# Attention and gated mixer on one core: P.V in bursts of two waves, seven P slots beside in-place VectorE tiles, the polynomial in halves, and unread products on TensorE

## The chip, the cores and the metric

The kernel runs on one core of one Trainium2 chip. The metric is device time in microseconds (us) of one execution, as the median of several runs. The core has four engines that matter here: TensorE (PE in the profile; PEld is its weight load), VectorE (DVE), ScalarE (ACT) and GpSimd (POOL); SyncE (SP) issues transfers. Each engine works through its own instructions in order, and semaphores tie the engines together.

## The reference: what is computed

Two branches over the same 2048 x 512 input x, mixed by a gate per row. All tensors are bfloat16.

```
A:  q = x @ wq (32 heads of 16),  k = x @ wk,  v = x @ wv      (one k and v for all heads)
    p = softmax(q k^T / 4),  a = concat(p v) @ wo
B:  z = gelu(x @ w_in);  z1 = z[:, :688];  z2 = layernorm(z[:, 688:])
    b = (z1 * (w_sp @ z2 + b_sp)) @ w_out
out = g * a + (1 - g) * b,   g = sigmoid(sum(x * gate_w))
```

The bulk is branch A: 32 heads x 2048 x 2048 scores, their exponentials, and the products of these with v.

## The kernel before

**Units and blocks.** The heads and queries are cut into 32 units. A unit takes four groups g (0 to 3) of 32 partitions, each group with its own head's 512 queries, against 2048 keys in 16 tiles of 128. That makes 64 blocks a unit, 2048 in all, each of 128 keys x 512 queries. For one block:

- TensorE makes the scores (`s_mm`): 32 rows of the array by 128 columns; blocks of different g run side by side as one wave, up to four.
- The exponential is taken by ScalarE, or by VectorE with a polynomial.
- TensorE multiplies by v (`pv_mm`): 128 rows by 32 columns, again up to four blocks of different g in a wave, summed for the unit in PSUM bank BO.

All matmuls with a tile position are issued on line 276, full ones (128 x 128) on line 275.

**ScalarE's path.** Steps alternate between three and two blocks, in two sets of PSUM banks (three banks, two banks). Line 539 takes the exponential of a whole step into one of NP = 5 slots of the tile P. A slot is free again when P.V has read its blocks.

**VectorE's path.** It takes blocks in batches of four. Each block's scores come through one PSUM bank, BD. Line 563 (`d_A`) reads the bank, scales and shifts it into a quarter of X. After four such steps the whole batch goes through three instructions (`d_poly`): line 570 squares X in place, line 571 adds a constant in place, line 572 squares X into the tile PD. The result is the polynomial's value; a correction per unit (two waves of products with MC and CC) makes good what the polynomial leaves out. X has NX = 3 slots, PD has ND = 4. A new batch (`new_batch`) starts only if the third last batch is computed and the fourth last is read by P.V.

**The end of a unit** (`norm`): VectorE transposes bank BO (line 582), takes the reciprocal of the sums (583), multiplies (585, 586) and after every second unit transposes the result (590). The next unit's P.V waits for line 582, since BO is single.

**The other work** ("misc"): projections, the two halves of z, the mixing with w_sp, and the output products. All of it goes through one PSUM bank, BM, in groups: a few full products, then one VectorE instruction that empties the bank. ScalarE's gelu passes run in one stretch, once all of z is there; in that stretch no exponentials run.

**What sets the order.** The order of each engine's instructions is fixed when the program is built. A planner steps through time with estimated costs: at each moment it takes, for the engine that is free first, the ready candidate with the lowest priority number. On TensorE these are the scores of ScalarE's next step (0), P.V under pressure (0.5), scores for VectorE alone (1), P.V or a correction (2), misc (3). Scores for VectorE's bank are added to the wave of ScalarE's step where the bank is free, or go alone if ScalarE's next step isn't due "soon". P.V goes if at least four blocks are ready, if the oldest unread P slot is about to hold up ScalarE ("press"), or if the unit is at its end ("last"). On VectorE the order is emptying of BM, `norm`, other work, `d_A`, polynomial. How many batches VectorE gets is not set by hand: it follows from the plan, within limits per unit (at most seven batches of a unit's 16). When the chip is slower than the plan's costs, the order stays and the semaphores make the engines wait.

## Time and profile before

| | us |
|---|---|
| median of 3 runs | 876.12 (874.2 to 879.94) |
| the profiled execution's own time | 871.82 |
| its span, first to last instruction | 870.0 |
| mean granted TensorE clock | 0.92 |
| busy: TensorE, ScalarE, VectorE | 798.3, 810.5, 665.8 |
| batches of four on VectorE | 89 |

The profile is of one execution. A row of a group reads: line, engine, operation, tile written <- tiles read, shapes, count | busy us, mean ns of one | idle time of the engine before them, and what ended it. A line of a timeline reads: start, length, engine, line, operation, tiles, count of instructions that are merged into it. A window reads: from:to, length, then busy time and count for each engine, the granted TensorE clock (1.00 is full speed), and DMA. Ends of matmuls are modelled, so the distance from start to start says more than the length. Since a window counts each instruction that touches it, counts at its edges are rough.

### The profile page before, as it was taken

What the parts mean: (1) busy time and instruction counts of PE and PEld (TensorE: products, weight loads), DVE (VectorE), ACT (ScalarE), POOL (GpSimd) and SP (SyncE); (2) the same over time, 40 slices, a digit from 0 to 9 for tenths busy, and PEclk for the clock granted to TensorE, in tenths of its full rate; (3) what the DMA queues carried; (4) which work ended last, traced back from release to release, by engine and by line L of the source; (5) the groups of instructions that cost most, each with busy time, mean ns of one, the idle gap of its engine ahead of it and who ended that gap; (6) DMA issues with size and microseconds to landing.
All of it is one profiled execution on the core that took longest, in us unless ns stands there. A gap on an engine that the chain in (4) does not pass through costs nothing.

```text
span 870.0 us, 13369 instructions
## 1 busy us (share of the span) xinstructions
PE 798.3 (92%) x5270; PEld 228.7 (26%) x5347; DVE 665.8 (77%) x1014; ACT 810.5 (93%) x698; POOL 10.9 (1%) x17
## 2 busy tenths in 40 slices
PE   8989999999990999999999999999989999999996
PEld 2222322222220122222222222222222222221222
DVE  3678888788989876877887888878668777867662
ACT  6889999999999789999999999999999999999893
POOL 2000000000000100000000000000000000000000
PEclk9789999999995599999999999999979999995757
DMA  9600000000000000004000031000050000000000
GB/s 235 119 1 1 1 2 1 1 2 2 1 1 0 2 1 1 1 6 105 13 2 1 1 80 36 7 2 1 1 98 13 13 1 1 2 1 1 1 2 28
DMA packets 49048, 16.98 MB, mean 20 GB/s; under 512 B 44129, under 2 KB 48913, under 8 KB 48978
## 3 DMA queue, kind: packets, MB, share of 16 engines
q1 hardware_dynamic: 46210, 15.23, 7.9%
q8 instruction: 44, 0.72, 0.4%
q10 hardware_dynamic: 2640, 0.56, 0.3%
q0 software_dynamic: 128, 0.26, 0.2%
q14 instruction: 26, 0.21, 0.1%
HBM read 3.20 MB, written 2.10 MB: 6 GB/s over the span
## 4 chain that ended last, share of the span: by engine, by line
PE 64%; DVE 25%; issue 6%; ACT 4%; ACTq 0%
PE ps L276 44%; PE ps L275 20%; DVE X L563 6%; DVE X L570 4%; ACT P L539 4%; DVE PD L572 3%; DVE bst L467 2%; DVE X L571 2%; DVE T L582 1%; DVE z L453 1%; DVE Tn L586 1%; DVE QA L341 1%; DVE z L477 1%; DVE OT L590 1%; DVE z L446 0%
## 5 line engine op out<-in xcount | busy, mean ns | idle before, releaser
L539 ACT ACTIVATE P<-ps 128x1536 bf16<-128x1536 f32 (+1 forms) x677 | 784.2, 1245 | 37.9 <-PE ps L276 32.7
L276 PE MATMUL ps<-QA,KA 32*128 32x512 bf16 x2048 | 327.3, 408 | 43.4 <-DVE X L563 23.5
L563 DVE TENSOR_SCALAR X<-ps 128x512 f16<-128x512 f32 x356 | 243.8, 685 | 131.6 <-PE ps L276 131.3
L276 PE MATMUL ps<-P,V 128*32 128x512 bf16 x1692 | 285.1, 416 | 2.0 <-DVE T L582 1.2
L276 PEld LDWEIGHTS ps<-QA,KA 32*128 32x128 bf16 x2048 | 78.5, 92 | 282.7 <-ACT P L539 120.7
L275 PE MATMUL ps<-wT,z 128*128 128x512 bf16 x351 | 113.9, 390 | 3.6 <-issue 2.9
L570 DVE TENSOR_TENSOR X<-X 128x2048 f16<-128x2048 f16 x89 | 108.9, 1223 | 2.6
L572 DVE TENSOR_TENSOR PD<-X 128x2048 bf16<-128x2048 f16 x89 | 108.7, 1221 | 1.9
L276 PEld LDWEIGHTS ps<-P,V 128*32 128x32 bf16 x1692 | 67.1, 94 | 163.4 <-issue 155.3
L571 DVE TENSOR_SCALAR X<-X 128x2048 f16<-128x2048 f16 x89 | 61.0, 685 | 0.6
L276 PE MATMUL ps<-PD,V 128*32 128x512 bf16 x356 | 46.3, 418 | 5.7 <-DVE PD L572 4.4
L275 PEld LDWEIGHTS ps<-wT,z 128*128 128x128 bf16 x384 | 29.6, 98 | 58.2 <-issue 51.0
L582 DVE STREAM_TRANSPOSE T<-ps 128x512 f32<-128x512 f32 x32 | 22.7, 711 | 16.9 <-PE ps L276 16.9
L275 PE MATMUL ps<-win,xT 128*128 128x344 bf16 x128 | 30.3, 315 | 2.5 <-DVE z L453 1.3
L275 PE MATMUL ps<-wout,z 128*128 128x512 bf16 x87 | 27.1, 392 | 1.4 <-issue 0.7
L275 PE MATMUL ps<-xT,win 128*128 128x512 bf16 x87 | 26.7, 384 | 1.6 <-DVE z L446 0.5
L500 DVE TENSOR_TENSOR z<-ps,z 128x512 bf16<-128x512 f32 (+1 forms) x24 | 16.4, 683 | 6.0 <-PE ps L276 4.2
L276 PE MATMUL ps<-QA,MC 128*32 128x512 bf16 x128 | 20.0, 428 | 0.5 <-DVE ct L422 0.5
L276 PE MATMUL ps<-ones,CC 128*32 128x512 bf16 x128 | 19.8, 427 | 0.0
L275 PE MATMUL ps<-xT,wq 128*128 128x512 bf16 x55 | 17.9, 385 | 1.1 <-DVE z L453 0.6
L275 PE MATMUL ps<-wo,OT 128*128 128x512 bf16 x59 | 18.6, 384 | 0.0
L446 DVE CAST z<-ps 128x512 bf16<-128x512 f32 x24 | 16.4, 683 | 1.7 <-PE ps L275 1.7
(97 smaller groups left out, 265.0 us busy)
## 6 DMA issues: line engine op xcount, KB each, us to landing
out_dram<-outsb SPq DMA_DIRECT2D x16, 128.0 KB, 1.7
win<-in_B_w_in_dram SPq DMA_DIRECT2D x2, 688.0 KB, 5.5
wout<-in_B_w_out_dram SPq DMA_DIRECT2D x1, 640.0 KB, 9.0
wo<-in_A_wo_dram SPq DMA_DIRECT2D x1, 512.0 KB, 6.6
wq<-in_A_wq_dram ACTq DMA_DIRECT2D x1, 384.0 KB, 7.4
wT<-in_B_w_sp_dram SPq DMA_TRANSPOSE x16, 4.5
KA<-KA POOLq DMA_DIRECT2D x4, 64.0 KB, 2.7
wq<-in_A_wq_dram ACTq DMA_DIRECT2D x1, 128.0 KB, 3.9
```

Of the source, the lines that this page charges most:

```text
L275: return t.matmul(dst, lhsT, rhs, start=start, stop=stop)
L276: return t.matmul(dst, lhsT, rhs, start=start, stop=stop, tile_position=tp)
L341: [(620, lambda: op("dve", lambda v: v.tensor_copy(QA[:, qt % NQ, :], bank(BM)), r=[BMK], w=[("Q", qt % NQ)], tag="Qev"))],
L446: ev = lambda: op("dve", lambda v: v.tensor_copy(z1[:, ft, 512 * tc:512 * tc + 512], bank(BM)), r=[BMK], w=[("z1", ft)], tag="z1ev")
L467: dve_q.append((440, lambda st=st, h=h: op("dve", lambda v: v.bn_stats(bst[:, st, h, :], z2[:, FH * st + 344 * h:FH * st + 344 * h + 344]) ...
L500: ev = lambda: op("dve", lambda v: v.tensor_tensor(dst, ps[0:n, 512 * BM:512 * BM + 512], dst, ALU.mult), r=[BMK, ("z1", ft)], w=[("u", ft ...
L539: op("act", lambda a: a.activation(P[:, k % NP, 0:512 * n], ps[:, 512 * b0:512 * (b0 + n)], ACT.Exp), r=[("sc", k % 2)], w=[("P", k % NP)] ...
L563: op("dve", lambda v: v.tensor_scalar(X[:, m % NX, 512 * i:512 * i + 512], bank(BD), PA, PB, ALU.mult, ALU.add), r=[("bk", BD)], w=[("X", ...
L570: (C2, lambda: op("dve", lambda v: v.tensor_tensor(x, x, x, ALU.mult), r=[k], w=[k], tag="dU")),
L571: (C4, lambda: op("dve", lambda v: v.tensor_scalar(x, x, PC, None, ALU.add), r=[k], w=[k], tag="dV")),
L572: (C2, lambda: op("dve", lambda v: v.tensor_tensor(PD[:, m % ND, :], x, x, ALU.mult), r=[k], w=[("PD", m % ND)], tag="dW")),
L582: res = [(660, lambda: o("dve", lambda v: v.transpose(T1[:], bank(BO)), r=[("bk", BO)], w=["T1"], tag="T1"), setT(("O", u)))]
```

## The change

1. **P.V in bursts of two waves.** P.V goes if eight blocks are ready (PVMIN), no longer four. "Press" now sets in when NP - PRESS = 6 slots back is reached (five slots unread), with NP = 7; before it was NP - 2 = 3 (two slots unread).
2. **Seven P slots; VectorE's tiles in place.** P goes from 5 to 7 slots. PD is gone: the last step of the polynomial writes bfloat16 over the float16 values it reads, in X, which has 5 slots. A new batch starts if the fifth last is read.
3. **The polynomial in halves.** Each of the three instructions over 2048 elements becomes two over 1024, in the order square, square, add, add, last square, last square. X is tracked by halves, and the first half's two blocks can go to P.V ahead of the second's.
4. **The plan's costs.** A TensorE candidate is charged 105 ns where its kind (S scores, P P.V, M full products) differs from the one before; before, it was 100 for each S and P and 60 in front of misc. The costs of VectorE's polynomial are those of the halves. "Soon" is 300 ns, no longer 500.
5. **Unread products.** `load` keeps for the last 3400 ns of the plan how much of the array the matmuls used (a full product of 512 columns counts 1, a score or P.V product 1/4). If TensorE has nothing to do within 100 ns, bank BM is free and the sum is under KEEP = 6.5, `keep_pick` issues a product of ones with ones into BM that nobody reads. While the gelu passes run, it also waits for the newest VectorE instruction.

```diff
-NP = 5
-NX = 3
-ND = 4
+NP = 7
+NX = 5
...
+PVMIN = 8
+PRESS = 1
+SOON = 300
+KEEP = 6.5
...
-        PD = sb("PD", [128, ND, 512 * DB], B16)
...
-        def mm(dst, lhsT, rhs, start, stop, r, w, tp=None, tag=""):
+        def mm(dst, lhsT, rhs, start, stop, r, w, tp=None, tag="", after=()):
...
+            load.append((T["now"], lhsT.shape[0] * sh[0] * n / (128.0 * 128 * 512)))
+            return op("pe", fn, r=r, w=w, after=after, tag=tag)
...
-        C512, C344 = 220.0, 150.0
-        C4, C2 = 80 + 0.26 * 512 * DB, 75 + 0.5208 * 512 * DB
+        C512, C344 = 218.0, 148.0
+        SW = 105.0
+        C4, C2 = 40 + 0.26 * 256 * DB, 30 + 0.5208 * 256 * DB
...
         def d_poly(m):
-            x = X[:, m % NX, :]
-            k = ("X", m % NX)
-            return [
-                (C2, lambda: op("dve", lambda v: v.tensor_tensor(x, x, x, ALU.mult), r=[k], w=[k], tag="dU")),
-                (C4, lambda: op("dve", lambda v: v.tensor_scalar(x, x, PC, None, ALU.add), r=[k], w=[k], tag="dV")),
-                (C2, lambda: op("dve", lambda v: v.tensor_tensor(PD[:, m % ND, :], x, x, ALU.mult), r=[k], w=[("PD", m % ND)], tag="dW")),
-            ]
+            res = []
+            hw = 512 * DB // 2
+            pair = [(X[:, m % NX, hw * h:hw * h + hw], ("X", m % NX, h), X[:, m % NX, hw * h:hw * h + hw].bitcast(B16), ("X", m % NX, h)) for h in range(2)]
+            for x, k, p_, kp in pair:
+                res.append((C2, lambda x=x, k=k: op("dve", lambda v: v.tensor_tensor(x, x, x, ALU.mult), r=[k], w=[k], tag="dU")))
...
-            if m >= NX and bdone.get(m - NX) is None:
-                return False
-            if m >= ND and pd_left.get(m - ND, 0) > 0:
+            if m >= NX and pd_left.get(m - NX, 0) > 0:
                 return False
...
+        def sw(kind):
+            return 0.0 if last_pe["kind"] == kind else SW
...
-                    soon = t < now + 500
+                    soon = t < now + SOON
...
-                    press = st_["ke"] + 1 - oldest >= NP - 2
+                    press = st_["ke"] + 1 - oldest >= NP - PRESS
...
-                    if pick and (len(pick) >= 4 or press or last):
+                    if pick and (len(pick) >= PVMIN or press or last):
...
-                        cands.append((now, prio, 100 + 216 * nw, emit3, fin3))
+                        cands.append((now, prio, sw("P") + 216 * nw, emit3, fin3, "P"))
...
-                tl = tail_pick(now)
+                tl = tail_pick(now) or keep_pick(now)
...
+        def keep_pick(now):
+
+            while load and load[0][0] < now - 3400:
+                load.popleft()
+            if sum(w_ for _, w_ in load) >= KEEP or misc["cur"] is not None or misc["free"] + LAT > now or tl_state[12] or st_["pu"] >= NU:
+                return None
+
+            def emit():
+                after = [pg.ops["dve"][-1]] if gel_on and gel else []
+                mm(bank(BM), ones[:, 0:128], ones[:], True, True, ["ones"], [BMK], tag="keep", after=after)
+            return (now, 9, C512 + sw("M"), emit, None, "M")
```

## The prediction

> **What bounds the kernel now.** I read the page's busy rows and groups first, then the table of waits, then the windows by stage.

> ```profile
> PE 798.3 (92%) x5270; PEld 228.7 (26%) x5347; DVE 665.8 (77%) x1014; ACT 810.5 (93%) x698; POOL 10.9 (1%) x17
> L539 ACT ACTIVATE P<-ps 128x1536 bf16<-128x1536 f32 (+1 forms) x677 | 784.2, 1245 | 37.9 <-PE ps L276 32.7
> L276 PE MATMUL ps<-P,V 128*32 128x512 bf16 x1692 | 285.1, 416 | 2.0 <-DVE T L582 1.2
> L563 DVE TENSOR_SCALAR X<-ps 128x512 f16<-128x512 f32 x356 | 243.8, 685 | 131.6 <-PE ps L276 131.3
> ```

> ScalarE is busy 93% of the span, nearly all of it in 677 exponentials for 1692 score blocks: 784.2/1692 = 0.463 us a block. VectorE does the other 356 blocks by the polynomial, 89 batches of four, and stands idle 131.3 us in front of its first step because TensorE has not delivered the block. So the time is ScalarE's, and the way to shorten it is to let VectorE take more blocks, which TensorE prevents.

> The windows by stage (per stage: length, then busy time and count on PE, weight loads, DVE, ACT, POOL; granted clock, DMA):

> ```profile
> 0.00:52.00 52.00, 45.01 (x286) 14.26 (x289) 29.35 (x66) 37.53 (x35) 7.98 (x16) 0.80 0.68 148
> 52.00:260.00 208.00, 195.17 (x1374) 58.94 (x1388) 173.05 (x263) 203.16 (x180) 0.00 (x0) 1.00 0.00 1
> 260.00:284.00 24.00, 1.77 (x6) 0.38 (x6) 21.98 (x55) 23.94 (x14) 0.14 (x1) 0.57 0.00 0
> 284.00:310.00 26.00, 24.75 (x111) 4.91 (x115) 20.05 (x36) 17.82 (x16) 2.79 (x1) 0.55 0.01 1
> 310.00:778.00 468.00, 451.02 (x3070) 131.29 (x3124) 364.16 (x515) 457.33 (x396) 0.00 (x0) 0.99 0.08 18
> 778.00:855.00 77.00, 72.33 (x400) 15.89 (x398) 53.55 (x77) 69.41 (x60) 0.00 (x0) 0.61 0.00 1
> 855.00:870.00 15.00, 8.24 (x37) 2.99 (x33) 3.69 (x7) 1.31 (x3) 0.00 (x0) 0.84 0.13 41
> ```

> In the long stages ScalarE is 97.7% busy, VectorE 83% and 78%, TensorE 94 to 96%. From 284 to 310 and from 778 to 855 the granted clock is 0.55 and 0.61, and there ScalarE loses 8.2 and 7.6 us, though TensorE looks busy.

> **The bursts of P.V.** TensorE's timeline in the warm middle:

> ```profile
> 407.21 0.39 PE L276 MATMUL ps<-QA,KA 32*128 32x512 bf16 x3
> 407.53 0.40 PE L276 MATMUL ps<-P,V 128*32 128x512 bf16 x3
> 407.86 0.60 PE L275 MATMUL ps<-wo,OT 128*128 128x512 bf16 x2
> 408.40 0.39 PE L276 MATMUL ps<-QA,KA 32*128 32x512 bf16 x2
> 408.72 0.40 PE L276 MATMUL ps<-PD,V 128*32 128x512 bf16 x4
> 408.94 0.39 PE L276 MATMUL ps<-P,V 128*32 128x512 bf16 x2
> ```

> A wave of scores, of P.V, or one full product takes 0.22 us behind its own kind (408.72 to 408.94) and 0.32 behind another (407.21 to 407.53): a change of kind costs 0.10. Each exponential's two or three P.V products now go out alone: 677 waves at 0.32, 217 us, and 89 waves of PD at 0.22, 20 us. In pairs of full waves it is 2048/8 = 256 bursts of 0.10 + 2 x 0.22 = 0.54, 138 us. That frees up to 99 us; with leftovers at the 32 unit ends I count 80. ScalarE doesn't gain from it by itself: in the long stages it is 97.7% busy. What it buys is the 131.3 us of VectorE's wait.

> **The polynomial in halves, in place.** VectorE's timeline beside it, the polynomial's groups, and a short product for the fixed cost:

> ```profile
> 403.97 0.68 DVE L563 TENSOR_SCALAR X<-ps 128x512 f16<-128x512 f32 x1
> 404.69 1.22 DVE L570 TENSOR_TENSOR X<-X 128x2048 f16<-128x2048 f16 x1
> 405.83 0.68 DVE L563 TENSOR_SCALAR X<-ps 128x512 f16<-128x512 f32 x1
> 406.43 0.68 DVE L571 TENSOR_SCALAR X<-X 128x2048 f16<-128x2048 f16 x1
> 407.15 1.23 DVE L572 TENSOR_TENSOR PD<-X 128x2048 bf16<-128x2048 f16 x1
> ```

> ```profile
> L570 DVE TENSOR_TENSOR X<-X 128x2048 f16<-128x2048 f16 x89 | 108.9, 1223 | 2.6
> L572 DVE TENSOR_TENSOR PD<-X 128x2048 bf16<-128x2048 f16 x89 | 108.7, 1221 | 1.9
> L571 DVE TENSOR_SCALAR X<-X 128x2048 f16<-128x2048 f16 x89 | 61.0, 685 | 0.6
> L333 DVE TENSOR_TENSOR sq<-QA 128x512 bf16<-128x512 bf16 x16 | 6.5, 408 | 0.1
> ```

> Writing in place is free: L570 (in place) and L572 (into PD) take the same. An instruction whose successor doesn't need it gives way before its end (404.69 to 405.83 is 1.14 for a 1.22; 405.83 to 406.43 is 0.60), one whose successor needs it does not (406.43 to 407.15, 0.72). Halves: (1223 - 408)/1536 = 0.531 ns an element, so 0.68 us for 1024, less 0.08 for the early start, 0.60; the add, with the same fixed part, (685 - 136)/2 + 136 = 0.41, less 0.08, 0.33. In the new order each half stands behind one it doesn't need, so a batch is 4 x 0.60 + 4 x 0.60 + 2 x 0.33 = 5.46 us. If no start were early it is 4 x 0.68 + 4 x 0.68 + 2 x 0.41 = 6.26. What a batch costs now:

> ```profile
> 52.00:260.00 208.00, 126.51 (x156) 1.00 0.00 1
> 284.00:310.00 26.00, 12.03 (x15) 0.55 0.01 1
> 310.00:778.00 468.00, 299.95 (x373) 0.99 0.08 18
> 778.00:855.00 77.00, 48.25 (x59) 0.61 0.00 1
> ```

> (VectorE's work on tile X alone, seven instructions a batch.) From 310 to 778 it is 299.95/(373/7) = 5.63. I take 5.46, nearest to the rows of independent neighbours, and keep 6.26 as the other end.

> [...]

> **More blocks for VectorE.** A batch now needs the third last batch's tile computed and the fourth last's read; then, the fifth last's read. That is looser, with a shorter hold by the halves. I let VectorE reach 93% busy (83 and 78 now; above 93 every late block hits ScalarE's queue of work), its other work unchanged per us: 46.5/208 = 22% and 64/468 = 14%. From 310 to 778: (0.93 - 0.14) x 4/5.46 = 0.579 blocks per us against 213/468 = 0.455; ScalarE stays at 0.977/0.463 = 2.11. Together 2.69 for 2.57: 468 becomes 447, **-21**. From 52 to 260: 0.52 for 0.43, **-7**. VectorE's scores may now go if ScalarE's next step isn't due within 0.3 us, not 0.5; a wave of 0.32 then delays that step by little, and ScalarE's other PSUM buffer covers it. No DMA is moved.

> **Unread products.** The weight loads on TensorE in steps of 3.41 us (each line: busy time and count, granted clock, DMA), and then, for one of these steps, only the full products and their loads, of which there are none:

> ```profile
> 819.49:822.90 3.41, 0.64 (x16) 1.00 0.00 0
> 822.90:826.32 3.42, 0.74 (x20) 0.51 0.00 0
> 826.32:829.73 3.41, 0.66 (x21) 0.50 0.00 0
> 829.73:833.14 3.41, 0.73 (x17) 0.99 0.02 5
> 833.14:836.56 3.42, 0.76 (x20) 0.51 0.01 2
> ```

> ```profile
> 822.90:826.32 3.42, 0.00 (x0) 0.00 (x0) 0.51 0.00 0
> ```

> A score or P.V product uses a quarter of the array (32 x 128 or 128 x 32 in its row). After a step with 16 or 17 the clock falls, after 20 it stays low, after 21 it rises: the line lies near 5 full products' worth per step. The change fills up to 6.5. So 284-310 and 778-855 should run at 1.00. At 2.11 plus VectorE's 0.63 blocks per us, the 184 blocks of the last stage (69.41/0.463 + 59/7 x 4) take 67 us, **-10** (5.5 of it from the clock alone); the 47 blocks of 284-310 at about 2.45 take 19, **-7**. Start and end: a cold start with two more P slots, **-1**, between 0 and -5. Products go only where the plan has TensorE idle over 0.1 us; one costs 0.22 + 0.10 and another 0.10 back. Unhidden it delays a score wave by 0.4, inside ScalarE's mean step of 784.2/677 = 1.16, as its other buffer is full.

> In the gelu stretch each product also waits for VectorE's newest instruction; behind it stand the next VectorE block's scores and P.V. TensorE works 1.77 of those 24 us and ScalarE runs gelu, so this is hidden; if VectorE lags there, the first exponentials start late, by 0 to 3 us.

> [...]

> **Sum.** 21 + 7 + 10 + 7 + 1 = 46 off the profiled execution's 871.8: 826. The runs' median, 876.1, lies 4 above it: **830**.

> **Rivals.** (B) The bursts hold VectorE's tiles and P.V back, or VectorE is late for other work, and it takes no more blocks: only the clock pays, 7 + 5.5 = 12 off: 864. For it: the wait of 131.3 us is for scores, partly behind one single PSUM bank, which stays single. Against: TensorE's 80 free us. 15%.
> (C) A batch costs 6.26, and the plan, which cannot see it, gives out as many batches as in the forecast: 0.579 x 447 + 0.52 x 201 + 0.63 x 67 + 22 at the start and around the gelu is 427 blocks, 107 batches; 107 x 6.26 = 670, other work 665.8 - 89 x 5.63 = 165, idle ends 52 - 29.35 + 15 - 3.69 = 34: 869; with 6, from the span of 870.0 to the median, 875. 7%.
> (D) The products don't hold the clock where TensorE is busy anyway: the last stage stays, 840. 9%.
> (E) Slower: ScalarE runs out of P slots at each unit's change. The next unit's P.V waits for the last burst and the transpose below, and only two of seven slots are kept free (three of five before).

> ```profile
> L582 DVE STREAM_TRANSPOSE T<-ps 128x512 f32<-128x512 f32 x32 | 22.7, 711 | 16.9 <-PE ps L276 16.9
> ```

> Two slots cover 2 x 1.16 = 2.3 us; burst 0.54, half 0.60 in front and transpose 0.71 make 1.85. It decides if a change takes 1.8 us longer than that cover: 31 x 1.8 = 56, 886. 7%.

> My forecast has 62%. The range, 806 to 865, goes down by VectorE at 97% (-9) and the start's and end's full gain, and up to B; C and E lie outside. Chances, with 1% the least that can be told: faster 84% (forecast, D, most of B), same 8% (C, the rest of B), slower 8%.

> **What would show it.** P.V rows in bursts of eight at 0.54; VectorE's wait for ps in front of its first step well under 131 us and its instructions on X at about 107 batches; ScalarE's exponentials near 1621/2.5 = 650; half products 0.60 apart; clock 1.00 after the gelu and in the last stage. Wrong: VectorE's batches still near 89, ScalarE idle behind P.V at unit changes, or a clock still at 0.5 with products in every step.

## The result

| | before | the change |
|---|---|---|
| median of four runs, us | 876.04 (874.2 to 879.94) | 850.86 (841.8 to 853.02) |
| ratio | | 0.9687, 95% interval 0.961 to 0.9765 |
| profiled execution: own time, span | 871.8, 870.0 | 853.0, 851.2 |
| granted clock of that execution | 0.920 | 0.927 |
| batches of four on VectorE | 89 | 108 |

The change is faster by 3.1%, and the medians lie 25 us apart; 46 were forecast. In another comparison, below, the same kernel gained only 1.4% (ratio 0.9864, 0.9812 to 0.9916); its four runs lie at 849.45, 859.99, 863.04 and 869.27 us, and the last two, over 1.5% above the first, count as slow. So the gain is real, and its size moves from one comparison to the next.

### The profile page after: what moved, and what is told of

It is laid out like the page before. It is cut to its first block, busy times and chain, and to the rows that moved or that the text cites. A ratio compares the mean times of both kernels' runs of the same rounds, so it can differ in the third digit from the quotient of the medians.

```text
span 851.2 us, 13946 instructions
## 1 busy us (share of the span) xinstructions
PE 789.3 (93%) x5416; PEld 209.9 (25%) x5416; DVE 765.5 (90%) x1471; ACT 776.0 (91%) x668; POOL 10.9 (1%) x17
## 4 chain that ended last, share of the span: by engine, by line
DVE 54%; PE 34%; issue 7%; ACT 3%; DMA 2%; SPq 0%; ACTq 0%
PE ps L278 22%; DVE X L572 20%; PE ps L277 12%; DVE X L580 9%; DVE X L584 7%; DVE X L582 5%; ACT P L548 2%; DVE T L594 2%; DVE bst L476 2%; DVE z L455 1%; DMA KA<-KA 1%; DVE Tn L598 1%; DVE z L462 1%; DMA xT<-in_A_x_dram 1%; DVE z L509 1%
## 5 line engine op out<-in xcount | busy, mean ns | idle before, releaser
L548 ACT ACTIVATE P<-ps 128x1536 bf16<-128x1536 f32 (+1 forms) x647 | 749.6, 1244 | 52.3 <-PE ps L278 48.1
L278 PE MATMUL ps<-QA,KA 32*128 32x512 bf16 x2048 | 364.1, 406 | 33.6 <-DVE X L572 16.4
L572 DVE TENSOR_SCALAR X<-ps 128x512 f16<-128x512 f32 x432 | 294.3, 681 | 39.4 <-PE ps L278 38.1
L278 PE MATMUL ps<-P,V 128*32 128x512 bf16 x1616 | 168.7, 412 | 0.0
L278 PEld LDWEIGHTS ps<-QA,KA 32*128 32x128 bf16 x2048 | 87.8, 91 | 326.4 <-ACT P L548 128.9
L584 DVE TENSOR_TENSOR X<-X 128x1024 bf16<-128x1024 f16 x216 | 144.1, 680 | 0.0
L580 DVE TENSOR_TENSOR X<-X 128x1024 f16<-128x1024 f16 x216 | 141.9, 680 | 0.0
L582 DVE TENSOR_SCALAR X<-X 128x1024 f16<-128x1024 f16 x216 | 84.0, 415 | 0.0
L278 PE MATMUL ps<-X,V 128*32 128x512 bf16 x432 | 71.4, 407 | 0.1
L278 PEld LDWEIGHTS ps<-P,V 128*32 128x32 bf16 x1616 | 33.7, 95 | 61.3 <-issue 57.8
L277 PE MATMUL ps<-ones 128*128 128x512 bf16 x81 | 32.4, 487 | 8.2 <-DVE bst L476 5.1
```

The costliest lines, as they stand in the source:

```text
L277: return t.matmul(dst, lhsT, rhs, start=start, stop=stop)
L278: return t.matmul(dst, lhsT, rhs, start=start, stop=stop, tile_position=tp)
L548: op("act", lambda a: a.activation(P[:, k % NP, 0:512 * n], ps[:, 512 * b0:512 * (b0 + n)], ACT.Exp), r=[("sc", k % 2)], w=[("P", k % NP)] ...
L572: op("dve", lambda v: v.tensor_scalar(X[:, m % NX, 512 * i:512 * i + 512], bank(BD), PA, PB, ALU.mult, ALU.add), r=[("bk", BD)], w=[("X", ...
L580: res.append((C2, lambda x=x, k=k: op("dve", lambda v: v.tensor_tensor(x, x, x, ALU.mult), r=[k], w=[k], tag="dU")))
L582: res.append((C4, lambda x=x, k=k: op("dve", lambda v: v.tensor_scalar(x, x, PC, None, ALU.add), r=[k], w=[k], tag="dV")))
```

## The profile after

The page of the changed kernel: the busy row, the granted clock in 40 slices, and groups (columns as in the profile before). Its lines are numbered anew: 548 is the exponential, 572 VectorE's first step on a block, 580, 582 and 584 are the polynomial's square, add and last square, 277 and 278 the matmuls, 476 VectorE's statistics for the layernorm, 1111 ScalarE's part of the output.

```profile
PE 789.3 (93%) x5416; PEld 209.9 (25%) x5416; DVE 765.5 (90%) x1471; ACT 776.0 (91%) x668; POOL 10.9 (1%) x17
PEclk8759996899999889999999999999998999999757
...
L548 ACT ACTIVATE P<-ps 128x1536 bf16<-128x1536 f32 (+1 forms) x647 | 749.6, 1244 | 52.3 <-PE ps L278 48.1
...
L572 DVE TENSOR_SCALAR X<-ps 128x512 f16<-128x512 f32 x432 | 294.3, 681 | 39.4 <-PE ps L278 38.1
...
L277 PE MATMUL ps<-ones 128*128 128x512 bf16 x81 | 32.4, 487 | 8.2 <-DVE bst L476 5.1
```

VectorE has taken the blocks that it was meant to take: 432 first steps, 108 batches, for 89 (forecast 107). ScalarE has 647 exponentials left, for 677 (forecast 650), and its busy time fell from 810.5 to 776.0, by 34.5 us. VectorE's wait for scores in front of a block fell from 131.3 to 38.1 us. All this came as forecast. Yet the span fell by 18.8 us only: ScalarE was idle for 59.5 us of the old span (870.0 - 810.5) and is idle for 75.2 of the new one (851.2 - 776.0). Its wait for scores grew from 32.7 to 48.1. The other open point is the clock: 81 unread products were issued (12 of them as warm-up, as before), and the clock is hardly better.

The windows of the changed kernel (per stage: length, busy time and count on PE, weight loads, DVE, ACT, POOL; granted clock, DMA):

```profile
30.00:62.00 32.00, 30.21 (x163) 6.68 (x159) 21.80 (x46) 23.22 (x22) 0.97 (x2) 0.52 0.24 46
...
133.00:157.00 24.00, 23.93 (x121) 4.56 (x122) 17.45 (x31) 16.60 (x14) 0.00 (x0) 0.50 0.00 1
...
799.00:840.00 41.00, 35.81 (x206) 7.32 (x207) 29.72 (x55) 32.02 (x29) 0.00 (x0) 0.55 0.00 1
```

The stretch behind gelu is warmer than before (0.75 from 284 to 310, for 0.55), but the last stage stayed near half speed (0.55). The cold stretch near the start is longer (30 to 62; before, from 31 to 52 with a break of 3 us), and one is new: 133 to 157. In that one TensorE is busy 23.93 of 24.00 us, and ScalarE loses 7.4.

The timelines of the changed kernel. First VectorE, then TensorE, in the warm middle, then the place behind gelu:

```profile
399.77 0.42 DVE L582 TENSOR_SCALAR X<-X 128x1024 f16<-128x1024 f16 x1
400.11 0.68 DVE L509 TENSOR_TENSOR z<-ps,z 48x512 bf16<-48x512 f32 x1
400.71 0.67 DVE L572 TENSOR_SCALAR X<-ps 128x512 f16<-128x512 f32 x1
401.31 1.27 DVE L584 TENSOR_TENSOR X<-X 128x1024 bf16<-128x1024 f16 x2
402.51 0.68 DVE L572 TENSOR_SCALAR X<-ps 128x512 f16<-128x512 f32 x1
...
401.48 0.61 PE L278 MATMUL ps<-P,V 128*32 128x512 bf16 x8
402.03 0.38 PE L278 MATMUL ps<-QA,KA 32*128 32x512 bf16 x1
...
306.11 3.39 PE L277 MATMUL ps<-ones 128*128 128x512 bf16 x7 [1.20 <-DVE bst L476]
313.31 8.23 ACT L548 ACTIVATE P<-ps 128x1536 bf16<-128x1536 f32 x7 [3.88 <-PE ps L278]
```

Two half squares take 402.51 - 401.31 = 1.20, so 0.60 each, and a half add takes 400.11 - 399.77 = 0.34. A burst of eight P.V products takes 402.03 - 401.48 = 0.55. These are the forecast's prices. The last two lines show a place where the unread products may hurt: seven of them, each held back for VectorE's statistics, stand in front of scores behind gelu, and ScalarE then waits 3.88 us. Without any products, in the first experiment below, it waits there for 2.91 us, so at most about 1 us of this is theirs.

## The experiments

Two theories were set against each other. **Clock theory:** the missing time was lost because the unread products didn't hold the clock. **Plan theory:** the order of the instructions was written with too low a price for VectorE's halves, so VectorE runs late against it, and TensorE's queue, which holds the scores for both engines in one fixed order, makes ScalarE wait too. The plan's price for a half square is 30 + 0.5208 x 1024 = 563 ns, for a half add 40 + 0.26 x 1024 = 306; the trace shows 600 and 335. In a batch that is 4 x 37 + 2 x 29 = 206 ns, in 108 batches 22 us that the plan doesn't know of.

**Without the unread products.**

```diff
-KEEP = 6.5
+KEEP = 0
```

> The changed kernel without the unread products (KEEP = 0), all else as changed. Clock theory (the 21 us that the change did not save are ScalarE's idle time in cold stretches that the products do not reach: they go only where the plan has TensorE idle, and none is issued after 788 us): the products warm only the gelu stretch and about 30 us behind it, and cost a 3.9 us wait there, so without them the time rises by 0 to 8 us, to 851-859, mean granted clock 0.88 to 0.91. Rival, the forecast's account (the products hold the clock and save about 12 us): 863 or more, clock below 0.88. VectorE theory (VectorE, 96% busy in the middle, is now the bound): no change, 849-854.

Measured: 848.43 us (844.87 to 851.75), ratio 0.9711 (0.9662 to 0.976). That is the changed kernel's time: the products as they are bring nothing that can be measured. Their conditions explain it. They go only where the plan has TensorE idle and bank BM free, and none goes any more once the final output groups hold BM (`tl_state[12]` in `keep_pick`). In the trace nearly all stand between 285 and 318 and between 768 and 788, only one in the cold stretch of 30 to 62 (at 33.2), none in that of 133 to 157 and none after 788. Behind gelu, where they do stand, they hold the clock: from 284 to 325 us it is 0.83 with them and 0.50 without.

**Products where they are needed.** In front of each of ScalarE's scores, where the plan's load of the last 3400 ns is under 7, one unread full product goes into the bank that the scores are about to overwrite.

```diff
+FILL = 7.0
...
+                        if thin:
+                            b0 = EB[k % 2][0]
+                            mm(bank(b0), ones[:, 0:128], ones[:], True, True, ["ones"], [bkey(b0)], tag="fill")
```

> The changed kernel with one more unread full product in front of a ScalarE step's scores, into the bank that these overwrite, wherever the plan's load of the last 3.4 us is under 7.0, whether TensorE is idle or not. Clock theory: granted clock 0.97 or more, the cold stretches at 30-62, 133-157 and 799-840 us gone with some 20 to 25 of ScalarE's 30 idle us in them, less delays of single waves: 828 to 838, ratio to the kernel before 0.945 to 0.957. VectorE theory: the clock rises but the time stays within 845 to 855, with VectorE above 92% busy. If the line of the clock lies above 7, the clock stays under 0.95.

Measured: 836.73 us (829.63 to 839.24), ratio 0.9552 (0.9485 to 0.962), granted clock of the profiled execution 0.976; one stretch, 36 to 57, is still cold at 0.51. So the clock can be held this way, and the edit was worth about 14 us here, not the whole gap. The products have a price in the plan, so the order changes with them (106 batches for 108): not all of the 14 us need be the clock's.

**The same on the kernel before.** The edit above, with the counter `load`, and nothing else of the change.

```diff
...
+            load.append((T["now"], lhsT.shape[0] * sh[0] * n / (128.0 * 128 * 512)))
...
+                        if thin:
+                            b0 = EB[k % 2][0]
+                            mm(bank(b0), ones[:, 0:128], ones[:], True, True, ["ones"], [bkey(b0)], tag="fill")
```

> The kernel before, with nothing changed but the product in front of thin score waves (threshold 7.0 by the same sum over 3.4 us). What the clock alone is worth on the old kernel: the prediction's sum has 5.5 us for the last stage and 7 us behind the gelu, together 12: 862 to 866, granted clock 0.96 or more. If less than 4 us come, the cold stretches there were not what held ScalarE up.

Measured: 862.16 us (858.7 to 866.75), ratio 0.9845 (0.98 to 0.9891), clock 0.963. The edit is worth about 13 us on the old kernel; the prediction's rival B had put the clock at 12, of which 7 behind gelu and 5.5 in the last stage. The sum fits better than its parts: counted by blocks as below, the profiled execution is 7.6 us sooner in the last stage and 0.4 around gelu.

**P.V sent as before.** Bursts of four again, and "press" as early as before; slots, halves and products stay.

```diff
-PVMIN = 8
-PRESS = 1
+PVMIN = 4
+PRESS = 4
```

> The changed kernel with P.V as before (goes with four ready blocks, pressed when two slots are unread): PVMIN = 4, PRESS = 4; slots, halves, products and costs stay. Forecast's account (TensorE's time freed by the bursts is what gives VectorE its blocks): VectorE's batches fall from 108 to 93, TensorE is 94% occupied again in the middle, VectorE waits for scores again over 90 us, time 865 to 880. Rival (the slots and halves give the gain, the bursts none): 848 to 856 with the batches back near 93 but less idle time of ScalarE.

Measured: 863.87 us (861.21 to 872.13), ratio 0.987 (0.9834 to 0.9905), with 93 batches. Its busy row on the page, and then its waits:

```profile
PE 802.3 (93%) x5304; PEld 236.6 (27%) x5391; DVE 691.1 (80%) x1321; ACT 797.9 (92%) x692; POOL 10.9 (1%) x17
```

```profile
DVE X L572 <- PE ps L278: 96.4, 112, 2.8
ACT outsb L1111 <- PE ps L277: 25.5, 1, 25.5
```

Without the bursts VectorE is back at a wait of 96.4 us for scores, and 15 batches are lost. The bursts also pay in a second place, which the prediction didn't name: the last line is ScalarE waiting 25.5 us behind its last exponential for the output products, which TensorE had not got to. In the changed kernel this wait is 10.3 us.

**The polynomial in whole instructions,** in place, without and with the fill product (98 and 97 batches).

```diff
-            for x, k, p_, kp in pair:
-                res.append((C2, lambda x=x, k=k: op("dve", lambda v: v.tensor_tensor(x, x, x, ALU.mult), r=[k], w=[k], tag="dU")))
...
+            res.append((75 + 0.5208 * 512 * DB, lambda: op("dve", lambda v: v.tensor_tensor(x, x, x, ALU.mult), r=ks, w=ks, tag="dU")))
```

> The changed kernel with the polynomial in three whole instructions of 2048, in place, the plan's costs for them as before. Halves matter (a dependent successor waits 0.12 us longer, a whole instruction holds up the next block longer): 98 batches instead of 108, 40 blocks more on ScalarE at 0.463 us are 18 us: 862 to 872. VectorE theory (VectorE is overcommitted at 108 batches): fewer batches unload it and the time stays at 848 to 856. Each whole instruction starts the next 1.14 us later if it is not needed, 1.26 if it is.

> The run with a product in front of thin score waves (threshold 7.0), with the polynomial in three whole instructions. With the clock out of the way, do the halves bring anything? Halves matter (106 against 97 batches, 36 blocks at 0.463 us): 850 to 856, about 17 us above the run with halves. VectorE theory (the extra batches are paid back by waits on an overcommitted VectorE): 836 to 843.

Measured: 851.29 us (849.67 to 864.97), ratio 0.9718 (0.9663 to 0.9773), without the fill; 845.25 (843.21 to 849.92), ratio 0.9657 (0.9626 to 0.9689), with it. Beside the halves, that is no difference without the fill and some 8 us with it (12 beside the next run, of the same comparison). So in the time of the kernel as changed, halves that put ten more batches on VectorE paid nothing. That they pay 7 us where the clock is full, and where these are lost, is shown below by counting blocks.

**What the products of the gelu stretch wait for:** the fill kernel, with these products tied to ScalarE's gelu in place of VectorE's newest instruction.

```diff
-                after = [pg.ops["dve"][-1]] if gel_on and gel else []
+                after = [pg.ops["act"][-2]] if gel_on and gel else []
```

> The run with a product in front of thin score waves (threshold 7.0), and the unread products of the gelu stretch wait for ScalarE's second newest instruction in the plan in place of VectorE's newest. Wait theory (behind the gelu, ScalarE stands idle about 4 us because its scores are queued behind products that wait for VectorE's late statistics): that idle time goes, 3 to 5 us less than the run with the wait on VectorE: 831 to 834, and no idle stretch of ScalarE over 2 us between 300 and 330 us. Rival (ScalarE would wait there for VectorE's own late work anyway): no change within 2 us, the idle time only moves.

Measured: 833.36 us (830.45 to 836.53), ratio 0.954 (0.9499 to 0.958). No difference that can be told from the fill kernel's: behind its second exponential after gelu ScalarE still stands idle for 4.12 us, and in the fill kernel for 4.02. So the idle time didn't come from what the products wait for.

**Fill and true prices.** The plan's two prices are set to what the trace shows.

```diff
-        C4, C2 = 40 + 0.26 * 256 * DB, 30 + 0.5208 * 256 * DB
+        C4, C2 = 65 + 0.26 * 256 * DB, 67 + 0.5208 * 256 * DB
```

> The run with a product in front of thin score waves (threshold 7.0), and the plan charges a half of the polynomial what the profile shows: 0.60 us a square, 0.33 us an add, in place of 0.56 and 0.31. VectorE theory (the plan overcommits VectorE, its late work holds up ScalarE by single waits): 104 batches instead of 106, 8 blocks more on ScalarE (+3.7 us), but ScalarE's idle time between 57 and 780 us falls by 6 us or more: 830 to 836. Rival (VectorE's lateness costs nothing): 838 to 842.

Measured: 824.91 us (822.42 to 829.71), ratio 0.9447 (0.9404 to 0.9491), with 104 batches. The plan gives VectorE two batches less than in the fill kernel, and the kernel is 12 us faster (8 us beside the run before, 833.36, which was in the same comparison, and whose interval lies clear of this one): the prices act by order, not by more work.

**True prices alone.** The same two prices, no fill product, 106 batches.

> The change with one thing edited: the plan's prices of VectorE's polynomial instructions set to what the trace of the changed kernel shows between the starts of neighbours (0.60 us for a half square, 0.33 us for a half add, in place of 0.56 and 0.31). Nothing is added on TensorE. Plan theory (VectorE runs late against the order written for it, and ScalarE pays in small gaps whatever the clock is): most of the 12 us of the run with fill product and prices come back here too, 838 to 843 us, ScalarE's idle time 10 us or more below the 75 us of the changed kernel, the clock still near 0.93. Rival (the prices only pay once the clock is warm, as the halves did): 848 to 853 us, idle time as before.

Measured: 826.29 us (819.21 to 834.0), ratio 0.9422 (0.9375 to 0.9468). This is more than either theory had expected (838 to 843, or 848 to 853). The change unaltered, in the same comparison, has 0.9864 (below), and the kernel with fill and true prices 0.9447: once the prices are true, the fill adds nothing that can be measured. Its page, busy row, clock and chain, and beneath it the chain of the changed kernel:

```profile
PE 744.9 (90%) x5339; PEld 205.3 (25%) x5421; DVE 753.4 (91%) x1451; ACT 773.3 (94%) x671; POOL 11.1 (1%) x17
PEclk8769999999999869999999999999999999999757
PE 41%; DVE 37%; issue 9%; ACT 9%; DMA 3%; SPq 0%; ACTq 0%; DVEq 0%
```

```profile
DVE 54%; PE 34%; issue 7%; ACT 3%; DMA 2%; SPq 0%; ACTq 0%
```

With true prices the chain that ends last goes through VectorE for 37% of the span instead of 54%. ScalarE's busy time hardly differs (773.3 for 776.0); its idle time falls from 75.2 to 824.0 - 773.3 = 50.7. And the last stage is as cold as in the changed kernel, by the last three figures of the clock row. The rival, that prices pay only with a warm clock, falls.

To keep the clock out of it altogether, take a stretch in which it is full in every kernel. The windows of the changed kernel, the fill kernel and the kernel with true prices, in this order:

```profile
320.00:630.00 310.00, 300.07 (x2171) 82.00 (x2171) 295.57 (x551) 298.76 (x259) 0.00 (x0) 1.00 0.08 18
```

```profile
320.00:630.00 310.00, 290.51 (x2099) 80.92 (x2136) 291.38 (x551) 298.35 (x259) 2.93 (x1) 0.99 0.08 18
```

```profile
320.00:630.00 310.00, 292.13 (x2187) 81.64 (x2226) 299.13 (x560) 306.36 (x268) 0.00 (x0) 1.00 0.12 25
```

The clock is 0.99 to 1.00 in all three. ScalarE is busy 298.76, 298.35 and 306.36 of the 310 us, in 259, 259 and 268 instructions: fill products do nothing here, true prices give 7.6 us. Some of this is where the stretch begins: the idle piece of 4.02 us behind gelu falls into it in the fill kernel, and one of 2.49 us, at 332.9, in the changed kernel. From 340 to 630 us ScalarE is busy 282.47, 282.64 and 286.68 us of 290, so the fill again does nothing, and true prices give 4.2. What gives way shows in the waits of the whole span (PEld is TensorE's weight load, which may wait while a matmul still runs: in front of the scores of the changed kernel the loads waited 326.4 us in all, the matmuls 33.6), of the changed kernel first, then of the one with true prices:

```profile
PEld ps L278 <- ACT P L548: 128.9, 292, 2.0
PEld ps L278 <- DVE X L572: 85.1, 216, 1.2
ACT P L548 <- PE ps L278: 48.1, 88, 3.9
```

```profile
PEld ps L278 <- ACT P L548: 166.6, 385, 1.3
...
PEld ps L278 <- DVE X L572: 60.8, 166, 1.5
...
ACT P L548 <- PE ps L278: 26.5, 42, 4.5
```

The weight loads' wait for VectorE to free bank BD (line 572) falls from 85.1 to 60.8 us, their wait for ScalarE rises from 128.9 to 166.6, as it should where ScalarE is the bound, and ScalarE's wait for scores falls from 48.1 to 26.5.

**The rest of VectorE's prices**, in the kernel with fill and true prices, and the gelu products tied to ScalarE.

```diff
-            res = [(660, lambda: o("dve", lambda v: v.transpose(T1[:], bank(BO)), r=[("bk", BO)], w=["T1"], tag="T1"), setT(("O", u)))]
-            res.append((210, lambda: o("dve", lambda v: v.reciprocal(rc[:].unsqueeze(2), t1[:, :, 16:17]), r=["T1"], w=["rc"], tag="rc"), None))
+            res = [(740, lambda: o("dve", lambda v: v.transpose(T1[:], bank(BO)), r=[("bk", BO)], w=["T1"], tag="T1"), setT(("O", u)))]
+            res.append((285, lambda: o("dve", lambda v: v.reciprocal(rc[:].unsqueeze(2), t1[:, :, 16:17]), r=["T1"], w=["rc"], tag="rc"), None))
...
```

> The run with fill product and polynomial prices (824.9 us), with the other VectorE prices of the plan set to the trace too (transpose of the output bank 0.74, reciprocal 0.285, its product 0.209, statistics 0.525 and 0.126), and the unread products of the gelu stretch waiting on ScalarE instead of VectorE. Plan theory: the idle piece of some 4 to 6 us behind gelu shrinks to under 2 us, and the time is 818 to 823 us. Rival (that piece is set by the order of the instructions, not by their prices): no change, 823 to 828 us, the idle piece over 3 us.

Measured: 825.4 us (817.81 to 832.42), ratio 0.9396 (0.9354 to 0.9438). The intervals of this and of the kernel with two true prices overlap. The idle piece behind gelu did get shorter, from 5.63 us to at most 1.46, but the stretch didn't. Windows of the kernel with fill and two true prices, then of this one:

```profile
290.00:330.00 40.00, 35.49 (x194) 8.24 (x195) 36.22 (x79) 33.28 (x29) 2.93 (x1) 0.83 0.00 0
```

```profile
290.00:330.00 40.00, 33.17 (x177) 7.53 (x180) 33.79 (x75) 32.84 (x28) 2.93 (x1) 0.74 0.00 0
```

ScalarE does 33.28 and 32.84 us of work in the same 40: one long piece was exchanged for several short ones. What holds ScalarE up there isn't settled.

**An eighth slot,** in that kernel.

```diff
-NP = 7
+NP = 8
```

> The run before, with eight P slots instead of seven and the wish to empty them (PRESS) beginning one slot later. Slot theory (the rival of the prediction in which ScalarE waits for a slot at unit changes still takes some us): ScalarE's remaining idle pieces at unit changes go, 3 us or more faster than the run with seven slots. Rival: the slots bind nowhere any more; within 2 us of that run, as 104 batches are planned in both.

Measured: 818.85 us (814.52 to 824.83), ratio 0.937 (0.9319 to 0.9421). The median is 6.6 us lower than with seven slots on the same chip, but the intervals of the ratios overlap by most of their length, so whether slots still bind is open. It has the lowest median of all, and against the kernel before and the change its interval is clear.

**The change again,** unaltered, beside the last three.

> The change unaltered, beside the three others on the same chip. If chips and days differ little: 846 to 853 us, a ratio of 0.966 to 0.974 to the kernel before, granted clock 0.92 to 0.95. If the clock of a run is set by when a stretch happens to go cold, times spread over 842 to 853 us with the clock going from 0.95 to 0.92.

Measured: 861.52 us (849.45 to 869.27), ratio 0.9864 (0.9812 to 0.9916). The four times 849.45, 859.99, 863.04 and 869.27 had granted clocks of 0.933, 0.915, 0.908 and 0.901, while the kernel before, on the same chip, ran between 870.31 and 880.55. So the changed kernel is the less steady of the two, and its time and its clock go together.

## Why the prediction was right in sign and too large

In each trace I counted how many of the 2048 blocks had their exponential done, on either engine (a VectorE block counts with its first step). Before, 85 were done at 52 us, 614 at 260, 760 at 346, 1867 at 778, and the last at 855.0. The table has how much sooner (-) or later (+) each profiled execution passed the stretches between these counts, in us. 614 to 760 holds gelu and what is around it. From 760 to 1867, the warm middle, the granted clock is 0.98 or more in every execution named here, so this row compares kernels without the clock. The forecast's 28 for both is 7 for the gelu stretch and 21 for the rest, which I share out by blocks.

| stretch | forecast | change | change again | + fill | + true prices | + both |
|---|---|---|---|---|---|---|
| start to block 85 | -1 | +0.5 | +1.6 | -2.0 | +3.4 | -2.5 |
| 85 to 614 | -7 | +5.7 | -6.4 | -1.3 | -10.3 | -6.8 |
| 614 to 760 | -8.7 | -3.3 | -1.3 | -6.1 | -5.4 | -4.3 |
| 760 to 1867 | -19.3 | -17.6 | -18.7 | -18.2 | -25.5 | -24.2 |
| 1867 to 2048 | -10 | -5.8 | +0.7 | -8.2 | -8.5 | -9.4 |
| last exponential to end | 0 | +1.7 | +1.7 | -0.7 | +0.3 | -1.7 |
| span | -46 | -18.8 | -22.3 | -36.5 | -46.0 | -48.8 |

The change's execution misses 27 of the 46 us. Only 1.7 of them are missing in the warm middle; 12.7 are between 85 and 614, 5.4 around gelu, 4.2 in the last stage, and 3.2 at the two ends.

**Bursts: right.** P.V goes out in 308 bursts (corrections counted) instead of some 690, 232 of them of exactly eight, at 0.55 us each, and VectorE's wait fell by 93 us. Taken back, they cost 13 us, but not where they were forecast to pay: in the warm middle the kernel with P.V as before takes 418.3 us for the change's 414.3 (VectorE does 0.500 blocks per us for 0.574, ScalarE 2.147 for 2.100), while the stretch behind the last exponential is 14.9 us longer.

**Halves: the price was right (0.60 and 0.34).** The gain is there in the warm middle, 414.3 us where whole instructions take 421.7 (413.7 and 420.5 with the fill); it doesn't show in the time of the kernel as changed because the profiled execution lost 12.2 us against whole instructions in the row 85 to 614, with its cold stretch. What halves bring with true prices wasn't run. The starts at 401.31 and 402.51 again lie ahead of the ends before them, by 0.07 us each (400.71 + 0.67 = 401.38, 401.31 + 1.27 = 402.58).

**"I let VectorE reach 93% busy" and ScalarE "stays at 0.977/0.463 = 2.11": right in the warm middle, partly by luck.** There ScalarE does 2.100 blocks per us and VectorE 0.574, where 2.11 and 0.579 were forecast. But VectorE is busy 95%, not 93, and ScalarE fell from 97.7 to 96.8%. I had written that above 93% every late block hits ScalarE, but took the plan to stop there. The plan believed a batch to be 0.21 us shorter than it is, so it filled VectorE to the brim. I had seen the mechanism, and put it only into rival C, for a batch of 6.26 "and the plan, which cannot see it"; I never compared the plan's prices in the diff with my own 0.60 and 0.33. With true prices VectorE does as much (0.578, at 96% busy), ScalarE reaches 98.8% and 2.146 blocks per us, and the row gives -25.5: what mattered was not the share of busy time but whether each instruction comes when the order expects it. So lateness costs some 8 us in this row, which my sum had not counted on.

**"So 284-310 and 778-855 should run at 1.00" is the step that failed.** I read that the change fills up to 6.5 and didn't read all conditions of `keep_pick`: in the last stage bank BM isn't free, and the -10 became -5.8, and +0.7 in the change again. Around gelu the products did warm the clock (0.92 from block 614 to 760, 0.75 in the kernel without them), but that saved under 1 us, 83.7 for 84.5: by this comparison, most of the 7 us that I gave to this stretch weren't the clock's. The new cold stretch, 133 to 157, I didn't foresee at all; with it the row 85 to 614 is +5.7 instead of -7. In the change again, the same program, the clock stayed full there, and the row is -6.4. The cold stretch starts where TensorE stood idle for VectorE, in the changed kernel's timeline:

```profile
131.70 0.39 PE L278 MATMUL ps<-QA,KA 32*128 32x512 bf16 x3
...
132.93 0.32 PE L277 MATMUL ps<-win,xT 128*128 128x344 bf16 x1 [0.84 <-DVE mx L356]
```

With true prices the profiled execution has no cold stretch between 54 and 272 us. That a late VectorE thins out TensorE's work and so lets the clock fall would explain why prices gave twice what I expected of them, and why fill and prices don't add up (0.9552 and 0.9422 alone, 0.9447 together). It is argued, not shown: in the change again VectorE's prices are as low, and the clock stayed full from 51 to 276 us; no run sets VectorE's lateness and the clock apart in such a stretch. Of the 27 us between the executions of the change and of true prices (851.2 and 824.0), 7.9 are in the warm middle and 16.0 between 85 and 614; against the change again (847.7) 6.9 are in the middle, 4.0 between 85 and 614, 4.1 around gelu and 9.2 in the last stage. That true prices reach the forecast's -46 to the us is luck: the middle gave more than forecast, and the last stage stayed cold.

**"5.5 of it from the clock alone", for the last stage: too much, once VectorE is on time.** With true prices alone the clock is at half speed for 31 of the 68.8 us that the last 181 blocks take; with fill and prices it is full and they take 67.9. In the change again, late and cold for 56 us, they take 78.0.

**Gelu stretch:** "the first exponentials start late, by 0 to 3 us": the third of them waited 3.88, and 2.91 in the kernel without products; before, there is one of 2.02 behind gelu. What sets it isn't settled.

**The rivals.** B (no more blocks) fell with 108 batches. C's mechanism was there, at 0.21 us a batch instead of 0.8. D (products don't hold the clock) is what happened to the products in the last stage, for another reason than D gave: none was issued there. Its 840 lies nearer to the measured 850.9 than the forecast's 830. E fell: of 31 unit changes, one shows a wait of ScalarE over 2 us (2.49 at 332.9).

## What to carry to other kernels

Where the order is written by a plan, compare every price in the plan with the distance from start to start in the trace, above all for an engine that the change fills up: with 37 ns more on a half square and 29 on a half add, and nothing else, the median went from 850.9 to 826.3 us; the fill alone brought it to 836.7. When an engine's busy time falls as forecast and the span doesn't, subtract one from the other first: the idle time that grew (59.5 to 75.2 us) says that work arrives late, not that there is too much of it. Then count what is done, stretch by stretch, and look at one with the same clock in every kernel: here it showed a middle that came as forecast and gains of halves and prices that the totals hid or blew up. A filler helps only where its conditions let it go, so look for it in the trace at the places that need it.
